# Attention in four joined pieces per unit, one piece per whole half step, and a fixed TensorE order in layer 1

## The chip, the cores and the metric

One core of a Trainium2 chip runs the whole program. The metric is the device time of one execution in microseconds; the time given for a kernel is the median of its runs.

## What is computed

Attention for 4 batches of 8 heads, 576 positions and head size 64, and behind it two feed-forward layers. The attention output of a head is the sum of two attentions: one over positions averaged by fours (144 of them), repeated four times, and one over a band of 7 positions around each query. The result, 2304 tokens by 512, goes through two layers with 2048 hidden columns each:

```python
out_d = sm_attn(q_d, k_d, v_d)                 # q, k, v averaged over 4 positions
out_up = np.repeat(out_d, factor, axis=2)
mask = np.abs(pos[:, None] - pos[None, :]) < factor
out_local = np.matmul(attn, v)                 # softmax over the masked scores
x = out_up + out_local
h = x @ w_in;  x = (h * sigmoid(1.702 * h)) @ w_out      # layer 1
h = x @ w_in;  x = elu(h) @ w_out                        # layer 2
```

All of it is float32. A product in float32 is made of three products of rounded halves (high by high, high by low, low by high), so each hidden block takes three matmuls where one would do.

## The kernel before

**Attention in units.** A unit is one batch and one pair of heads. There are 16; four of batch 0 are cut in two, and those and the four of batch 1 are computed in an opening whose order is written out token by token. This change is about the last eight, batches 2 and 3 (`rest[4:]`, called `turned`: their queries and keys are transposed on VectorE). A unit's work on TensorE is, by the names in the trace: `qk`, the banded scores in two PSUM tiles (5 and 4 windows); `qkd`, the averaged scores, two tiles; `pdt`, transposes of the averaged weights, two tiles; `ptr`, transposes of the banded weights, tiles of 4, 4 and 1 windows; `pvd`, averaged weights times values, one tile; `pv`, banded weights times values, two tiles (5 and 4 windows). VectorE masks and reduces the scores and adds the results into `x`, ScalarE takes the exponents (`exp_down` for `qkd`, three deferred groups of `exp_windows` for `qk`) and copies `pdT` and part of `PT`.

**PSUM.** In this part of the program every one of these tiles comes from the pool `spool`, tag `s`, which has two buffers, taken in turn. A tile can be written only when the tile two before it has been read by all its readers. For `qkd` the last readers are the exponents of `exp_down` on ScalarE (L630), which need `nmd`, made by two reductions (L609) and one scaling (L614) on VectorE.

**Layer 1 in steps.** Tokens go in blocks of 256 or 512; blocks 2 to 4 have 512 tokens and 16 steps each, a step being one column block f of 128 hidden columns. A step has two chunks: `products_h1` (12 matmuls of 128x512 into `h`, then tanh on ScalarE L1002, gate on VectorE L1006, rounding `g1h` L1012 and remainder `g1l` L1019) and `products_y1` of the step two before (12 matmuls into `y`). Each chunk is a generator that yields after each half of its matmuls. `step1` (L1276) goes through the chunks and at every yield calls `attend`, which first runs one deferred group of exponents and then one piece of attention from a queue:

```python
for chunk in chunks:
    for _ in chunk:
        ...
        with behind_step(si):
            for _ in range(rate(si)):
                attend()
```

So before there are four calls in a step. The queue is filled from `Unit.pieces` (L820 on): the front pieces of a unit (scores, averaged scores with `exps`, the transposing `turn` of the next unit), interleaved with the back pieces of the unit before (7 of them: `pdt` twice, `ptr` three times, `pv_down` with half of `pv`, the other half).

**What sets the order.** The code issues instructions in this order, and a scheduler of the language then places each engine's instructions by a model of when their operands are ready; `manual_schedule` keeps the written order for the engines that it names. The opening is under it for TensorE, ScalarE and VectorE. The steps behind it are under the scheduler for all engines, with `behind_step` (L953) as a bound: attention's instructions come behind the tanh and the gate of the last hidden block.

Of the kernel before, what the change touches and what calls it, by code (L numbers as in the profile page):

```python
# [24 lines left out]
NWIN = 9  # L25
# [10 lines left out]
FIRST = 4  # L36
# [9 lines left out]
}  # L46

RATE0 = 3
RATE1 = 1

LOADS = 6
NSIGN = 20
# [4 lines left out]
LAG = 2  # L57
# [51 lines left out]
OPENED = 16  # L109
# [9 lines left out]
def kernel(  # L119
# [275 lines left out]
    class Unit:  # L395
# [424 lines left out]
        def pieces(self):  # L820

            down = self.dn_from is None
            nxt = following.get(self)
            front = []
            if down and self not in turned:
                self.qkT, self.qkd = [None, None], [None, None]

                def k1():
                    self.trans(1, 1)
                    if nxt is not None and self not in early:  # L830
                        nxt.load_qk()

                front += [lambda: self.trans(0, 0), lambda: self.trans(0, 1), lambda: self.trans(1, 0), k1]
            elif not down:
                self.qkT = self.dn_from.qkT

            scores = [(lambda a=a: self.qk(a, min(a + 5, self.w1))) for a in range(self.w0, self.w1, 5)]
            if self in rest:
                scores = [lambda: (self.qk(0, 5), self.qk(5, self.w1))]
            front += scores  # L840
            if self in rest:
                front.append(lambda: (self.qk_down(0), self.qk_down(1), self.exps()))
                if nxt in turned:

                    front.append(nxt.turn)
                elif self in turned:
                    front.append(lambda: None)
            elif down:
                front += [lambda: self.qk_down(0), lambda: (self.qk_down(1), self.exps())]
            else:  # L850
                last = front.pop()
                front.append(lambda: (last(), self.exps()))

            def pv_last(a):
                self.pv(a, self.w1)
                if nxt is not None and self not in early:
                    nxt.load_v()

            back = []
            if down:  # L860
                back += [lambda: self.pdt(0), lambda: self.pdt(1)]
            back += [(lambda a=a: self.pt(a, min(a + 4, self.w1))) for a in range(self.w0, self.w1, 4)]
            starts = list(range(self.w0, self.w1, 5))
            if self in rest:
                back.append(lambda: (self.pv_down(), self.pv(0, 5)))
            else:
                if down:
                    back.append(self.pv_down)
                back += [(lambda a=a: self.pv(a, a + 5)) for a in starts[:-1]]
            back.append(lambda: pv_last(starts[-1]))  # L870
            return front, back

# [2 lines left out]
    rest = [Unit(b, hp, 0, NWIN) for b in range(1, B) for hp in range(NHP)]  # L875

    turned = rest[NHP:]
# [12 lines left out]
    back, back_of = [], None  # L890
# [9 lines left out]
    for u in rest[NREST:] + [None]:  # L900
        front, nback = pieces[u] if u is not None else ([], [])
# [11 lines left out]
        back, back_of = nback, u  # L913

    due = {}
# [27 lines left out]
    def split_some(blk):  # L943

        if blk < NBLK and nsplit[0] < NK * (blk + 1) and ready(blk):
            split_x(blk, nsplit[0] % NK)
            nsplit[0] += 1
# [4 lines left out]
    @contextmanager  # L952
    def behind_step(si):  # L953
        with ExitStack() as stack:
            if si >= WRITTEN:
                for ins in evacuated:
                    stack.enter_context(tc.issue_after(ins.ins))
            yield

    @contextmanager  # L960
    def behind_opening(si):
        with ExitStack() as stack:
            if si < OPENED + HELD:
                for ins in opened:
                    stack.enter_context(tc.issue_after(ins))
            yield
# [300 lines left out]
        released += [f"wo{f}" for f in (2 * (f2 - LAG), 2 * (f2 - LAG) + 1) if f >= 0]  # L1267
    used = set()

    def rate(si):  # L1270
        if due[1] and si < 8:
            return RATE0
        return RATE1

    waiting, prev, stage2, wextra = list(steps[OPENED - LAG:OPENED]), None, None, None
    def step1(si, blk, fs):  # L1276
        nonlocal prev, wt2, stage1, stage2, l1a, wextra, used
# [26 lines left out]
            hidden2(si - len(steps))  # L1304
        nchunk = 0
        for chunk in chunks:
            for _ in chunk:
                if not wt1.finished() and (blk == 0 or si < 3 * FIRST and si % 2 == 1):
                    wt1.convert()
                with behind_step(si):  # L1310
                    for _ in range(rate(si)):
                        attend()
                if blk == 0:
                    split_some(1)
                nchunk += 1
                if wt2 is not None and nchunk in (2, 3) and (nchunk == 2 or si % 2):
                    wt2.load(AHEAD + wt2.half - wt2.loaded)
                    with behind():
                        wt2.convert()
# [23 lines left out]
            wt2 = Weights(2, order2, stage2, 3, lambda tag: tag in used, 0)  # L1343
            wt2.load(AHEAD)

    for si, (blk, fs) in list(enumerate(steps + [(None, None)] * LAG))[OPENED:]:
        with behind_opening(si):
            step1(si, blk, fs)
    assert not queue
    l1.close()  # L1350

# [44 lines left out]
```

## Time and profile before

| | |
|---|---|
| time, 3 runs | 974.5, 975.35, 976.1 us (median 975.35) |
| profiled execution, own time | 974.49 us |
| span of that execution | 972.3 us |
| mean granted TensorE clock | 0.981 of full speed |
| busy: TensorE, VectorE, ScalarE, GpSimd | 948.0, 503.8, 466.6, 60.8 us |
| part with the units of batches 2 and 3 | about 195.5 to 376.9 us of the span |

How to read it: the profile comes from one execution. "PE" is TensorE's matmuls, "PEld" its weight loads, "DVE" VectorE, "ACT" ScalarE, "POOL" GpSimd. "L993" is line 993 of the kernel. In the views in order of time a row may stand for several like instructions (xN), and a matmul in float32 with plain operands (`qk`, `pv`, `ptr` and the like) appears as more than one record. Ends of matmuls are modelled; the distance between two starts is measured. Square brackets name what the engine waited for.

### The profile page before, as it was taken

Reading aid. Unit: us, or ns where it says so; the run is one execution under the profiler, and the core shown is the slowest. Engines: PE = TensorE matmul, PEld = TensorE weight load, DVE = VectorE, ACT = ScalarE, POOL = GpSimd, SP = SyncE. Lnnn points to the kernel's source line nnn. Section 1 sums busy time; section 2 is a strip of 40 time slices with the busy share of each in tenths; the row PEclk is TensorE's granted clock in tenths of the full one; section 3 lists DMA queues with packets and bytes.
Section 4 is the critical chain, followed back from the end, with each engine's and each line's share of the span. In section 5 each row is a group of like instructions: output and inputs, shape, how many; then the busy total and the mean of one; then the engine's idle time right before and its main releaser. Section 6 shows DMA issues by size and latency. Waiting matters only on the chain. (4 is left out here: it accounts for less than half of the span.)

```text
span 972.3 us, 14685 instructions
## 1 busy us (share of the span) xinstructions
PE 948.0 (97%) x5773; PEld 775.6 (80%) x5773; DVE 503.8 (52%) x900; ACT 466.6 (48%) x1115; POOL 60.8 (6%) x117
## 2 busy tenths in 40 slices
PE   8978999999999999999999999999999999999998
PEld 5758987777777778888888978877888888888897
DVE  5888997676654543223225898884223222322232
ACT  5667999464343532232225566664334333433343
POOL 4330110201111010000000000000000000000000
PEclk9588999999999999999999999999999999999999
DMA  9587712153222204010007921002001100100010
GB/s 192 162 232 205 232 31 55 46 116 64 52 55 46 70 20 144 1 43 1 1 1 240 366 88 43 1 12 77 1 1 38 39 1 1 55 0 1 1 44 22
DMA packets 113332, 67.97 MB, mean 70 GB/s; under 512 B 80752, under 2 KB 102768, under 8 KB 113264
## 3 DMA queue, kind: packets, MB, share of 16 engines
q1 hardware_dynamic: 110896, 66.46, 24.3%
q10 hardware_dynamic: 2368, 0.59, 0.4%
q8 instruction: 45, 0.74, 0.3%
q14 instruction: 23, 0.19, 0.1%
HBM read 57.59 MB, written 9.44 MB: 69 GB/s over the span
## 5 line engine op out<-in xcount | busy, mean ns | idle before, releaser
L1245 PE MATMUL o<-whl2o,g2h 128*128 128x512 f32 x576 | 181.0, 394 | 2.4 <-ACT ye L1072 2.1
L1196 PE MATMUL h<-x2h,whl2i 128*128 128x512 f32 (+1 forms) x640 | 159.3, 371 | 0.0
L1060 PE MATMUL y<-g1h,whl1o 128*128 128x512 f32 (+1 forms) x512 | 156.2, 371 | 0.0
L993 PE MATMUL h<-xh,whl1i 128*128 128x512 f32 (+1 forms) x640 | 147.1, 354 | 2.4 <-DVE g L1006 2.4
L1206 DVE SCALAR_TENSOR_TENSOR g<-e,h 128x512 f32<-128x512 f32 (+1 forms) x80 | 50.7, 634 | 177.9 <-ACT e L1204 177.6
L1196 PEld LDWEIGHTS h<-x2h,whl2i 128*128 128x128 f32 x640 | 114.7, 189 | 22.7
L1245 PEld LDWEIGHTS o<-whl2o,g2h 128*128 128x128 f32 x576 | 107.2, 189 | 27.1 <-ACT ye L1072 2.5
L993 PEld LDWEIGHTS h<-xh,whl1i 128*128 128x128 f32 x640 | 105.8, 190 | 19.4 <-DVE g L1006 3.3
L1203 ACT ACTIVATE e<-h 128x512 f32<-128x512 f32 (+1 forms) x80 | 44.3, 554 | 158.3 <-PE h L1196 158.3
L1245 PE MATMUL o<-whl2o,g2l 128*128 128x512 f32 x288 | 113.1, 393 | 0.0
L1060 PEld LDWEIGHTS y<-g1h,whl1o 128*128 128x128 f32 x512 | 92.4, 189 | 16.3 <-issue 1.2
L1006 DVE SCALAR_TENSOR_TENSOR g<-g,h 128x512 f32<-128x512 f32 x64 | 43.8, 684 | 118.9 <-ACT g L1002 118.9
L1002 ACT ACTIVATE g<-h 128x512 f32<-128x512 f32 x64 | 38.1, 596 | 122.7 <-PE h L993 115.9
L1060 PE MATMUL y<-g1l,whl1o 128*128 128x512 f32 (+1 forms) x256 | 93.7, 366 | 0.0
L1196 PE MATMUL h<-x2l,whl2i 128*128 128x512 f32 (+1 forms) x320 | 79.6, 370 | 0.0
L993 PE MATMUL h<-xl,whl1i 128*128 128x512 f32 (+1 forms) x320 | 77.6, 354 | 0.0
L1213 DVE TENSOR_TENSOR g2l<-g,g2h 128x512 fp32r<-128x512 f32 (+1 forms) x80 | 51.7, 646 | 36.8 <-ACT g2h L1211 21.6
L1211 ACT ACTIVATE g2h<-g 128x512 fp32r<-128x512 f32 (+1 forms) x80 | 47.1, 589 | 42.8 <-DVE g L1206 42.7
L1196 PEld LDWEIGHTS h<-x2l,whl2i 128*128 128x128 f32 x320 | 56.7, 188 | 11.0
L1245 PEld LDWEIGHTS o<-whl2o,g2l 128*128 128x128 f32 x288 | 54.4, 189 | 12.0
L993 PEld LDWEIGHTS h<-xl,whl1i 128*128 128x128 f32 x320 | 53.2, 191 | 7.3 <-issue 0.4
L1019 DVE TENSOR_TENSOR g1l<-g,g1h 128x512 fp32r<-128x512 f32 x64 | 44.2, 691 | 27.7 <-ACT g1h L1012 27.4
(128 smaller groups left out, 1326.2 us busy)
## 6 DMA issues: line engine op xcount, KB each, us to landing
wst1i<-in_moe_w_in_dram SPq DMA_DIRECT2D x16, 512.0 KB
wst1o<-in_moe_w_out_dram SPq DMA_DIRECT2D x16, 512.0 KB
wst2i<-in_moe_w_in_dram SPq DMA_DIRECT2D x16, 512.0 KB
wst2o<-in_moe_w_out_dram SPq DMA_DIRECT2D x16, 512.0 KB
vr<-in_v_dram SPq DMA_DIRECT2D x32, 144.0 KB
out_dram<-ot SPq DMA_DIRECT2D x18, 256.0 KB
y<-ydram SPq DMA_DIRECT2D x16, 256.0 KB
ydram<-ye SPq DMA_DIRECT2D x14, 256.0 KB
```

The source lines that it names most:

```text
L993: nc.tensor.matmul(out=hps[blk, fs][:, i, :], lhsT=w_in(1, f, c, wp), rhs=columns(xp, c), start=(n == 0), stop=(n >= len(todo) - nf), skip ...
L1002: return nc.scalar.activation(out=g, in_=hps[blk, fs], func=AF.Tanh, scale=0.851)
L1006: return nc.vector.scalar_tensor_tensor(out=g, in0=g, scalar=1.0, in1=ph, op0=ALU.add, op1=ALU.mult)
L1019: return nc.vector.tensor_tensor(out=gl, in0=g, in1=gh.bitcast(F32), op=ALU.subtract)
L1060: nc.tensor.matmul(out=sums(m), lhsT=w_out(1, f, wp)[:, m, :], rhs=gp[:, i, :], start=(opens and n == 0 and m % per == 0), stop=(last and ...
L1196: nc.tensor.matmul(out=ph[:, :n], lhsT=w_in(2, f, c, wp), rhs=xp[:, c, :n], start=(i == 0), stop=(i == 3 * NK - 1),)
L1203: nc.scalar.activation(out=e[:, :n], in_=ph[:, :n], func=AF.Relu, scale=-1.0)
L1206: urgent["dve"] = nc.vector.scalar_tensor_tensor(out=g[:, :n], in0=e[:, :n], scalar=-1.0, in1=ph[:, :n], op0=ALU.add, op1=ALU.max)
L1211: nc.scalar.activation(out=gh[:, :n], in_=g[:, :n], func=AF.Copy)
L1213: return lambda: nc.vector.tensor_tensor(out=gl[:, :n], in0=g[:, :n], in1=gh[:, :n].bitcast(F32), op=ALU.subtract)
L1245: nc.tensor.matmul(out=ops[bi][i], lhsT=gp[:, i * P:(i + 1) * P], rhs=wo[wp], start=(f == 0 and m == 0), stop=(f == NF - 1 and m == 2),)
```

## The change

The four parts: (1) a unit of batches 2 and 3 has two front pieces (`qk`; `qkd` with the exponents and the next unit's `turn`) and four back pieces (both `pdt`; `ptr` of 8 windows; `ptr` of the last window with `pvd`; all of `pv`), each of exactly two PSUM tiles. (2) `attend` is called once per chunk, behind its second half, so twice a step instead of four times. (3) The rate table and two calls that had nothing left to do in these steps (conversion of layer 1's weights, splitting of block 1) are gone. (4) All steps behind the opening are inside `manual_schedule` for TensorE: it keeps the written order, while ScalarE and VectorE are still placed by the scheduler.

```diff
@@ -44,9 +44,6 @@
     "qT": (3, "qs", 0), "sl": (3, "qs", 576),
     "kT": (4, "kd", 0), "qd": (4, "kd", 576), "kd": (4, "kd", 720),
 }
-
-RATE0 = 3
-RATE1 = 1
 
 LOADS = 6
 NSIGN = 20
@@ -839,12 +836,9 @@
                 scores = [lambda: (self.qk(0, 5), self.qk(5, self.w1))]
             front += scores
             if self in rest:
-                front.append(lambda: (self.qk_down(0), self.qk_down(1), self.exps()))
-                if nxt in turned:
-
-                    front.append(nxt.turn)
-                elif self in turned:
-                    front.append(lambda: None)
+                front.append(
+                    lambda: (self.qk_down(0), self.qk_down(1), self.exps(), nxt.turn() if nxt in turned else None)
+                )
             elif down:
                 front += [lambda: self.qk_down(0), lambda: (self.qk_down(1), self.exps())]
             else:
@@ -856,17 +850,19 @@
                 if nxt is not None and self not in early:
                     nxt.load_v()
 
+            if self in rest:
+                return front, [
+                    lambda: (self.pdt(0), self.pdt(1)), lambda: (self.pt(0, 4), self.pt(4, 8)),
+                    lambda: (self.pt(8, NWIN), self.pv_down()), lambda: (self.pv(0, 5), pv_last(5)),
+                ]
             back = []
             if down:
                 back += [lambda: self.pdt(0), lambda: self.pdt(1)]
             back += [(lambda a=a: self.pt(a, min(a + 4, self.w1))) for a in range(self.w0, self.w1, 4)]
             starts = list(range(self.w0, self.w1, 5))
-            if self in rest:
-                back.append(lambda: (self.pv_down(), self.pv(0, 5)))
-            else:
-                if down:
-                    back.append(self.pv_down)
-                back += [(lambda a=a: self.pv(a, a + 5)) for a in starts[:-1]]
+            if down:
+                back.append(self.pv_down)
+            back += [(lambda a=a: self.pv(a, a + 5)) for a in starts[:-1]]
             back.append(lambda: pv_last(starts[-1]))
             return front, back
 
@@ -1267,11 +1263,6 @@
         released += [f"wo{f}" for f in (2 * (f2 - LAG), 2 * (f2 - LAG) + 1) if f >= 0]
     used = set()
 
-    def rate(si):
-        if due[1] and si < 8:
-            return RATE0
-        return RATE1
-
     waiting, prev, stage2, wextra = list(steps[OPENED - LAG:OPENED]), None, None, None
     def step1(si, blk, fs):
         nonlocal prev, wt2, stage1, stage2, l1a, wextra, used
@@ -1304,14 +1295,10 @@
             hidden2(si - len(steps))
         nchunk = 0
         for chunk in chunks:
-            for _ in chunk:
-                if not wt1.finished() and (blk == 0 or si < 3 * FIRST and si % 2 == 1):
-                    wt1.convert()
-                with behind_step(si):
-                    for _ in range(rate(si)):
+            for half, _ in enumerate(chunk):
+                if half == 1:
+                    with behind_step(si):
                         attend()
-                if blk == 0:
-                    split_some(1)
                 nchunk += 1
                 if wt2 is not None and nchunk in (2, 3) and (nchunk == 2 or si % 2):
                     wt2.load(AHEAD + wt2.half - wt2.loaded)
@@ -1343,9 +1330,10 @@
             wt2 = Weights(2, order2, stage2, 3, lambda tag: tag in used, 0)
             wt2.load(AHEAD)
 
-    for si, (blk, fs) in list(enumerate(steps + [(None, None)] * LAG))[OPENED:]:
-        with behind_opening(si):
-            step1(si, blk, fs)
+    with tc.manual_schedule(engines={ET.PE}):
+        for si, (blk, fs) in list(enumerate(steps + [(None, None)] * LAG))[OPENED:]:
+            with behind_opening(si):
+                step1(si, blk, fs)
     assert not queue
     l1.close()
 
```

How the order moves, at three places. A name such as `pdt_2_2_0_3357` is tile, batch, pair of heads, first window and a buffer number; `h_2_8` is block 2, step 8.

TensorE, unit 2 of batch 2, from the last matmuls of the y chunk behind that unit's successor's `qkd`. Before:

```order
L1060 MATMUL y_2_2880<-g1h_4_3061,whl1o_1471 128x512
L1060 MATMUL y_2_2880<-g1l_4_3063,whl1o_1471 128x512
L1060 MATMUL y_2_2880<-g1h_4_3061,whl1o_1471 128x512
L993 MATMUL h_2_7_3300<-xh_2588,whl1i_1220 128x512 x2
L686 MATMUL pdt_2_2_0_3294<-ident,pd_2_0_3010 72x72 x4
L993 MATMUL h_2_7_3300<-xh_2588,whl1i_1220 128x512 x2
L993 MATMUL h_2_7_3300<-xl_2589,whl1i_1220 128x512 x2
L686 MATMUL pdt_2_2_0_3314<-ident,pd_2_0_3010 72x72 x4
L993 MATMUL h_2_7_3300<-xl_2589,whl1i_1220 128x512 x2
L993 MATMUL h_2_7_3300<-xh_2588,whl1i_1220 128x512 x4
```

With the change:

```order
L1056 MATMUL y_2_2841<-g1h_6_3140,whl1o_1652 128x512
L1056 MATMUL y_2_2842<-g1h_6_3140,whl1o_1652 128x512
L1056 MATMUL y_2_2842<-g1l_6_3142,whl1o_1652 128x512
L1056 MATMUL y_2_2842<-g1h_6_3140,whl1o_1652 128x512
L683 MATMUL pdt_2_2_0_3357<-ident,pd_2_0_3064 72x72 x4
L683 MATMUL pdt_2_2_0_3363<-ident,pd_2_0_3064 72x72 x4
L989 MATMUL h_2_9_3369<-xh_2590,whl1i_1456 128x512 x4
L989 MATMUL h_2_9_3369<-xl_2591,whl1i_1456 128x512 x4
L989 MATMUL h_2_9_3369<-xh_2590,whl1i_1456 128x512 x4
L701 MATMUL ptr_2_2_0_3393<-ident,sl_2_0_3017 70x128 x4
L701 MATMUL ptr_2_2_0_3399<-ident,sl_2_0_3017 70x128 x4
```

Before, each `pdt` stands alone between matmuls of the next `h`; now both stand together in front of the whole `h`, and both `ptr` tiles together behind it.

VectorE, from the gate of the hidden block that ends just ahead of `qkd` of unit 3 of batch 2 (its maxima `nmd`, the next unit's `qT` and `kT`). Before:

```order
L1006 SCALAR_TENSOR_TENSOR g_2_6_3235<-g_2_6_3235,h_2_6_3196 128x512
L609 TENSOR_REDUCE nmd_3_0_3242<-qkd_2_3_0_3244 72x2
L609 TENSOR_REDUCE nmd_3_0_3242<-qkd_2_3_0_3248 72x2
L1019 TENSOR_TENSOR g1l_6_3240<-g_2_6_3235,g1h_6_3238 128x512
L614 TENSOR_SCALAR nmd_3_0_3242<-nmd_3_0_3242 72x4
L532 STREAM_TRANSPOSE qT_0_0_3266<-rawq_0_0_3042 128x576
L522 TENSOR_REDUCE qd_0_0_3270<-qT_0_0_3266 128x144
```

With the change:

```order
L1002 SCALAR_TENSOR_TENSOR g_2_8_3301<-g_2_8_3301,h_2_8_3288 128x512
L606 TENSOR_REDUCE nmd_3_0_3308<-qkd_2_3_0_3310 72x2
L606 TENSOR_REDUCE nmd_3_0_3308<-qkd_2_3_0_3314 72x2
L529 STREAM_TRANSPOSE qT_0_0_3323<-rawq_0_0_3086 128x576
L1015 TENSOR_TENSOR g1l_8_3306<-g_2_8_3301,g1h_8_3304 128x512
L611 TENSOR_SCALAR nmd_3_0_3308<-nmd_3_0_3308 72x4
L529 STREAM_TRANSPOSE kT_0_0_3325<-rawk_0_0_3091 128x576
```

The transpose of the next unit's queries has moved ahead of the remainder `g1l` and of the scaling of `nmd`.

ScalarE, the first hidden block of block 3 (`pd` are the exponents that read `qkd`). Before (the exponents of this unit stand ahead of these rows):

```order
L1002 ACTIVATE g_3_0_4084<-h_3_0_4061 128x512
L623 ACTIVATE sl_2_0_3985,sumset<-sl_2_0_3985,nm_2_0_3986 128x70 x3
L1012 ACTIVATE g1h_0_4087<-g_3_0_4084 128x512
L694 ACTIVATE pdT_1_0_4071<-pdt_3_1_0_4098 72x288
L1002 ACTIVATE g_3_1_4124<-h_3_1_4104 128x512
L711 ACTIVATE PT_1_0_4111<-ptr_3_1_0_4131 70x512
L1002 ACTIVATE g_3_2_4153<-h_3_2_4137 128x512
```

With the change:

```order
L998 ACTIVATE g_3_0_4050<-h_3_0_4037 128x512
L998 ACTIVATE g_3_1_4093<-h_3_1_4080 128x512
L620 ACTIVATE sl_2_0_4011,sumset<-sl_2_0_4011,nm_2_0_4012 128x70
L1008 ACTIVATE g1h_0_4053<-g_3_0_4050 128x512
L620 ACTIVATE sl_2_0_4011,sumset<-sl_2_0_4011,nm_2_0_4012 128x70 x2
L627 ACTIVATE pd_2_0_4058,sumset<-qkd_3_2_0_4059,nmd_2_0_4057 72x144 x2
L627 ACTIVATE pd_2_0_4058,sumset<-qkd_3_2_0_4063,nmd_2_0_4057 72x144 x2
L691 ACTIVATE pdT_1_0_4103<-pdt_3_1_0_4104 72x288
```

The tanh of the second hidden block now stands ahead of the first block's rounding and of the four exponents that read `qkd`.

## Rows read from the trace of the kernel before

**Rows 1.** The page, part 1: TensorE's busy time, share of span, instructions.
```profile
PE 948.0 (97%) x5773; PEld 775.6 (80%) x5773; DVE 503.8 (52%) x900; ACT 466.6 (48%) x1115; POOL 60.8 (6%) x117
```

**Rows 2.** Stretches: busy time (instructions) by engine, then TensorE's clock, DMA.
```profile
195.50:376.90 181.40, 179.25 (x1377) 136.34 (x1378) 103.66 (x203) 81.44 (x298) 18.68 (x36) 1.00 0.27 58
400.00:500.00 100.00, 100.00 (x443) 82.81 (x442) 27.06 (x40) 26.52 (x45) 0.00 (x0) 1.00 0.03 11
```

**Rows 3.** Waits of TensorE, 195 to 377 us: total, times, longest.
```profile
PE h L993 <- DVE g L1006: 1.3, 2, 1.0
PE pdt L686 <- ACT pd L630: 0.5, 1, 0.5
PE qkd L602 <- DVE sl L577: 0.2, 1, 0.2
```

**Rows 4.** TensorE in order of time: start us, duration us, operation, count.
```profile
231.07 0.48 PE L1060 MATMUL y<-g1h,whl1o 128*128 128x512 f32 x1
231.38 0.40 PE L1060 MATMUL y<-g1l,whl1o 128*128 128x512 f32 x1
...
238.74 0.40 PE L1060 MATMUL y<-g1l,whl1o 128*128 128x512 f32 x1
239.07 0.33 PE L741 MATMUL pv<-PT,vw 70*64 70x64 f32 x2
239.32 0.73 PE L1060 MATMUL y<-g1h,whl1o 128*128 128x512 f32 x2
239.89 0.40 PE L1060 MATMUL y<-g1l,whl1o 128*128 128x512 f32 x1
```

**Rows 5.** Three engines in order of time, 246.5 to 251.8 us.
```profile
246.51 0.72 PE L602 MATMUL qkd<-kd,qd 64*72 64x144 f32 x8
...
246.96 0.60 ACT L1002 ACTIVATE g<-h 128x512 f32<-128x512 f32 x1 [8.14 <-PE h L993]
...
247.45 0.34 ACT L623 ACTIVATE sl<-sl,nm 128x70 f32<-128x70 f32 x1
...
248.19 0.81 DVE L609 TENSOR_REDUCE nmd<-qkd 72x2 f32<-72x288 f32 x2
...
248.46 0.62 ACT L1012 ACTIVATE g1h<-g 128x512 fp32r<-128x512 f32 x1
...
249.11 0.69 DVE L1019 TENSOR_TENSOR g1l<-g,g1h 128x512 fp32r<-128x512 f32 x1
...
249.72 0.43 DVE L614 TENSOR_SCALAR nmd<-nmd 72x4 f32<-72x4 f32 x1
...
250.04 0.61 PE L993 MATMUL h<-xh,whl1i 128*128 128x512 f32 x2
...
250.24 0.38 ACT L630 ACTIVATE pd<-qkd,nmd 72x144 f32<-72x144 f32 x1 [0.15 <-DVE nmd L614]
...
250.88 0.19 ACT L630 ACTIVATION_READ_ACCUMULATOR pd<-qkd,nmd 72x1 f32 x1
...
251.12 0.44 PE L686 MATMUL pdt<-ident,pd 72*72 72x72 f32 x4 [0.47 <-ACT pd L630]
...
251.59 0.20 ACT L630 ACTIVATION_READ_ACCUMULATOR pd<-qkd,nmd 72x1 f32 x1
```

**Rows 6.** VectorE by shape, 230 to 380 us: busy us, mean ns.
```profile
L532 DVE STREAM_TRANSPOSE qT<-rawq 128x576 f32<-128x576 f32 x4 | 3.1, 770 | 0.0
```

**Rows 7.** Order of time around the first unit of batch 2.
```profile
205.60 1.32 PE L559 MATMUL qk<-kT,qT 64*64 64x70 f32 x36
...
205.92 0.60 ACT L1002 ACTIVATE g<-h 128x512 f32<-128x512 f32 x1 [1.31 <-DMA ydram<-ye_both]
```

**Rows 8.** TensorE at the start of layer 2's output products.
```profile
576.48 0.73 PE L1245 MATMUL o<-whl2o,g2h 128*128 128x512 f32 x2 [2.07 <-ACT ye L1072]
```

**Rows 9.** Two stretches behind that wait, columns as in rows 2.
```profile
578.00:580.00 2.00, 2.00 (x6) 1.62 (x5) 1.86 (x3) 1.65 (x4) 0.00 (x0) 0.50 0.60 158
580.00:582.00 2.00, 2.00 (x7) 1.55 (x7) 2.00 (x5) 1.69 (x3) 0.00 (x0) 0.66 0.23 36
```

## The prediction

> **What bounds the kernel now.** The page's first part comes first: TensorE is busy for 97% of the span, VectorE and ScalarE for about half [rows 1]. So every microsecond that TensorE loses or gains counts, and nothing else does. Next the stretches: where only layer 1 runs, 100 us hold 443 matmuls of 128x512, 0.226 us each, with no idle time, and nothing can be won there; where the units of batches 2 and 3 are mixed in, 181.4 us of span, TensorE shows 179.25 us of work, while VectorE works 103.66 and ScalarE 81.44 us [rows 2]. Then the waits in that stretch: four in all, 2.0 us together [rows 3]. The reader is to see that waits are almost nothing today. What the stretch costs is attention's own matmuls and the changes between them and the dense matmuls.
>
> All times below are taken from the start of a piece on TensorE, and the sum is made against the profiled execution's own 974.49 us; the median of the runs is 975.35, 0.86 us above it, and the predicted time is moved up by that.
>
> **Term A: fewer changes of work on TensorE.** Counted in the order of time, TensorE turns to attention 83 times between 195.5 and 376.9 us. With six pieces in each of eight units it does so 48 times, 35 fewer. What one costs: behind four transposes (`pdt`) the two following dense matmuls start 0.31 us apart, 0.09 more than the 0.226 of an undisturbed pair; around two records of `pv` the start comes 0.33 us after a dense matmul (0.10 more) and the next two dense ones take 0.57 (0.12 more), so 0.22 [rows 4]. 35 times 0.09 is 3.2 us, 35 times 0.22 is 7.7. About half of the removed ones are transposes; I take 5 us gained.
>
> Here the row is at odds with a rule. The late start behind a piece is that of a dense matmul whose weights were not there yet. The Trainium skill (TensorE: Matmul & The Clock Gate, "Step-by-step: what each phase is for") says that TensorE pulls the next weight load ahead of the matmuls in flight where the row groups don't conflict or the load goes to the background buffer; by that a change would be hidden, term A would be nothing, and the kernel 5 us slower than I say. The rows price each change above zero, so I keep them.
>
> **Term B: the waits of before.** They hang on the old places of the pieces. All four go at most: 2.0 us gained [rows 3]; none goes at least. The places of the wait on `pd` and those on the gate are new, so I take 2.0.
>
> **Term C: new waits for the two PSUM buffers.** This decides. Every piece now fills both buffers of the pool, and TensorE keeps the written order, so it stands still until both are read. For five of the six pieces the readers are quick. Behind `qkd` they are not: its tiles are last read by four exponents on ScalarE, which need `nmd` scaled on VectorE, and on VectorE that scaling stands behind the gate, two reductions and the remainder `g1l`. The same chain stands in the trace of before [rows 5]: `qkd` starts at 246.51; the tanh of the block just finished at 246.96; the reductions at 248.19, `g1l` at 249.11, the scaling at 249.72 to 250.15; the exponents from 250.24. The second one's reading ends at 251.07, and `pdt` starts at 251.12, 4.61 us after `qkd`, having waited 0.47. With the change the transpose of the next unit's queries stands ahead of `g1l`, and takes 0.77 [rows 6]: 5.38. TensorE gets there after `qkd` and twelve dense matmuls, as it did at 250.04, 3.53 after [rows 5]. So it waits 1.8 us, and then again: the second buffer is free with the fourth exponent (251.79 in the rows, 0.72 after the second), while the first four transposes take only some 0.25. That is 0.47 more, 2.25 us a time.
>
> - Five times in this way (behind `qkd` of units 1 to 3 of batch 2, 0 and 1 of batch 3): 11.3 us. The first of them waits also for the weighing of unit 0; I add nothing for that.
> - Behind `qkd` of the last unit there is nothing to transpose: 2.25 less 0.77, 1.5 us.
> - Behind the first `qkd` (unit 0 of batch 2) the following piece is the next `qk`. Its tanh cannot start before 205.92, since its tile's last content is still on its way to memory [rows 7]; that wait is not on TensorE and stays. From there, by the durations of rows 5 and 6: tanh 0.60 and gate 0.69 to 207.2, reductions to 208.1, transpose to 208.8, `g1l` to 209.5, scaling to 210.0, two exponents with the reading (0.83) to 210.8. TensorE has the same work ahead of it as before and is there at 205.60 [rows 7]: 5.2 us.
> - In block 3 `qkd` of unit 2 is followed by a hidden chunk, and the tanh of that second block stands ahead of everything that the exponents need. It starts 3.53 plus 0.45 after `qkd`; then 0.60, one exponent 0.34, `g1h` 0.62, `g1l` 0.69, scaling 0.43, two exponents 0.83 [rows 5]: 7.5, less 3.53 is 4.0, with the second buffer 4.5 us.
>
> Together 22.5 us. Below: with the scaling placed as early as in the trace of before, 0.47 for the first buffer and 0.47 for the second, eight times, 7.5 us. Above: some 3 us more if the weighing of unit 0 and the second buffer in the first case bind. I take 22.5, since the order of the three engines is known and each duration has a row.
>
> **Term D: the clock.** A wait of 2.07 us on TensorE is in the trace of before [rows 8]. Behind it the granted clock was 0.50, 1.2 GHz, for 2 us, in which six matmuls stood instead of nine, and 0.66 on the mean of the next 2 [rows 9], which is 1.4 us more at the low level: of 3.4 us at half speed about 1.6 are lost. No wait of [rows 3], the longest 1.0, was followed by that: the clock there is 1.00 [rows 2]. The two waits of 4 us and over are longer than 2.07: 3.2 us. For the other six, 1.8 us with a short second one, the rows don't say: nothing at least, 9.6 us more at most. I take nothing, as none of them is 2.07 in one piece.
>
> Removing the rate table and the two calls costs and gains nothing: they issue no instruction in these steps. DMAs are the same in number. On SP's queue the four writes of block 0 and 1's result now stand together ahead of the next unit's queries, and the loads of values follow their pieces; the queries are needed three steps later, some 22 us, which covers them. If a load came late, `turn` would wait on VectorE, and with it the gate behind it.
>
> Sum: 974.5 - 5 - 2 + 22.5 + 3.2 = 993.2 us, and 994 against the median.
>
> **Rivals.** *The chain fits, and the kernel is faster.* VectorE is idle for 43% and ScalarE for 55% of the stretch [rows 2], so the buffers might be free when TensorE comes; then only A and B are left, 975.35 - 7 = 968 us. The point is whether the way from `qkd` to a free buffer is under 3.5 us. Against it: it was 4.6 before, without the transpose in it [rows 5]. *Half the waits.* The two long ones shrink to the regular size because engines at the head of a batch have run ahead, some regular ones to 1.8, and the clock stays up: 975.35 - 7 + 17 = 985 us. For it: TensorE's clock stayed at 1.00 through all of [rows 3]. *Every wait lowers the clock*: six times 1.6 more, 1004 us; for it, 1.8 and 0.47 us with a quarter of a microsecond of small transposes between them are close to the 2.07 of [rows 8]. *The change does not do what it says*: the written order might be undone, or the old one be as good as it; the printed order of TensorE has the joined pieces where the code puts them, so this is small: 975 us.
>
> **How the numbers follow.** The forecast, 988 to 999 us, has a chance of 0.40; half the waits 0.25; every wait with a low clock 0.19; faster 0.12; no change 0.04. 0.2%, 2 us, is about what a measurement of this kernel can tell from no change. The range is 978 to 1004: it leaves out the faster case, no change, and the far side of the low-clock case, about 0.2. Slower by over 0.2% is 0.84.
>
> **What would show it.** In the waits of TensorE `pdt` waiting for `pd` on ScalarE should appear seven times, most of 1.5 to 2 us in the first part and some 0.4 in the second, and `qk` for `pd` or `kT` once with about 5; attention should stand in 48 stretches; the granted clock should dip behind the two longest waits. It is wrong if `pdt` starts within 3.6 us of `qkd`, if the stretches between the pieces don't get shorter, or if the time beyond 400 us of the span changes other than by a shift.

## The result, and the profile after

The changed kernel takes 987.89 us, the median of four runs (987.49 to 989.49); the kernel before took 975.73 in the runs beside it. The ratio is 1.0129, 95% interval 1.0112 to 1.0147: slower, as forecast, inside the range, and 6 us below the point. The profiled execution took 987.54 us, its span is 985.8.

The page's first part, of the kernel after [rows 1]: TensorE's busy time is 2.3 us less than before, and its share is smaller.

```profile
PE 945.7 (96%) x5773; PEld 776.2 (79%) x5773; DVE 499.8 (51%) x900; ACT 466.7 (47%) x1115; POOL 67.1 (7%) x117
```

Stretches of the kernel after, columns as in [rows 2]. The one with the units of batches 2 and 3 is 199.5 us long, of which TensorE stands idle for 15.5 (2.2 before). The one behind it is as before: 0.226 us a matmul.

```profile
195.50:395.00 199.50, 184.04 (x1368) 142.91 (x1367) 103.93 (x208) 82.45 (x299) 25.57 (x36) 0.97 0.25 54
410.00:500.00 90.00, 90.00 (x399) 74.53 (x398) 24.70 (x37) 24.55 (x41) 0.00 (x0) 1.00 0.06 22
```

Waits of TensorE between 190 and 400 us in the kernel after, columns as in [rows 3]. All are for the readers of `qkd` or for the weighing of `pd` (VectorE multiplies the exponents by one over their sums, L662); the waits of before for the gate and for `sl` are gone.

```profile
PE pdt L683 <- ACT pd L627: 8.8, 12, 3.2
PE qk L556 <- ACT pd L627: 4.9, 1, 4.9
PE pdt L683 <- DVE pd L662: 1.8, 1, 1.8
```

One of the four regular places, in order of time [rows 5]. The transpose of the next unit's queries and `g1l` stand ahead of the scaling (248.25), the exponents follow at 248.50, and `pdt` starts at 249.38, 4.52 us after `qkd`, then waits again for the fourth exponent.

```profile
244.86 0.72 PE L599 MATMUL qkd<-kd,qd 64*72 64x144 f32 x8
245.03 0.60 ACT L998 ACTIVATE g<-h 128x512 f32<-128x512 f32 x1 [6.24 <-PE h L989]
...
246.26 0.81 DVE L606 TENSOR_REDUCE nmd<-qkd 72x2 f32<-72x288 f32 x2
...
246.53 0.62 ACT L1008 ACTIVATE g1h<-g 128x512 fp32r<-128x512 f32 x1
...
246.99 0.77 DVE L529 STREAM_TRANSPOSE qT<-rawq 128x576 f32<-128x576 f32 x1
247.68 0.64 DVE L1015 TENSOR_TENSOR g1l<-g,g1h 128x512 fp32r<-128x512 f32 x1
...
248.25 0.15 DVE L611 TENSOR_SCALAR nmd<-nmd 72x4 f32<-72x4 f32 x1
248.50 0.38 ACT L627 ACTIVATE pd<-qkd,nmd 72x144 f32<-72x144 f32 x1 [1.35 <-DVE nmd L611]
249.14 0.19 ACT L627 ACTIVATION_READ_ACCUMULATOR pd<-qkd,nmd 72x1 f32 x1
...
249.38 0.44 PE L683 MATMUL pdt<-ident,pd 72*72 72x72 f32 x4 [0.86 <-ACT pd L627]
...
250.10 0.44 PE L683 MATMUL pdt<-ident,pd 72*72 72x72 f32 x4 [0.28 <-ACT pd L627]
```

Where the time went. Between the same dense matmuls of both traces, one late in the opening and one behind the attention, the span grew by 12.3 us. The opening of this execution was 3.1 us longer (a load of values came later), and behind the attention it was 1.9 shorter; a second profile of the changed kernel (below) has the opening 1.0 shorter than before and the stretch 12.6 longer. So the opening is scatter, and the stretch is the change. The part behind the attention differs mainly by the clock: before, it fell behind the wait at the start of layer 2's output products [rows 8, 9]; in both profiles of the changed kernel it stayed at full speed there, behind 1.92 us in the first and 2.07 in the second (the rows of the second are in the last section).

In the stretch, attention's price is the distance between starts of dense matmuls over 0.227 us, added up: 58.5 us in 83 stretches before, 70.6 in 48 after. Of these 3.3 and 21.8 are waits and low clock; the pieces themselves cost 55.2 before and 48.8 (6.1 a unit) after.

### The profile page after: what moved, and what is told of

It reads as the page before. It is cut to its first block, busy times and chain, and to the rows that moved or that the text cites. A ratio compares the mean times of both kernels' runs of the same rounds, so it can differ in the third digit from the quotient of the medians.

```text
span 985.8 us, 14672 instructions
## 1 busy us (share of the span) xinstructions
PE 945.7 (96%) x5773; PEld 776.2 (79%) x5773; DVE 499.8 (51%) x900; ACT 466.7 (47%) x1115; POOL 67.1 (7%) x117
## 5 line engine op out<-in xcount | busy, mean ns | idle before, releaser
L1056 PE MATMUL y<-g1h,whl1o 128*128 128x512 f32 (+1 forms) x512 | 152.5, 368 | 0.0
L1192 PEld LDWEIGHTS h<-x2h,whl2i 128*128 128x128 f32 x640 | 114.3, 188 | 22.5
L989 PE MATMUL h<-xl,whl1i 128*128 128x512 f32 (+1 forms) x320 | 74.5, 353 | 0.0
L989 PEld LDWEIGHTS h<-xl,whl1i 128*128 128x128 f32 x320 | 55.5, 194 | 8.4
```

The source lines that it names most:

```text
L989: nc.tensor.matmul(out=hps[blk, fs][:, i, :], lhsT=w_in(1, f, c, wp), rhs=columns(xp, c), start=(n == 0), stop=(n >= len(todo) - nf), skip ...
L1056: nc.tensor.matmul(out=sums(m), lhsT=w_out(1, f, wp)[:, m, :], rhs=gp[:, i, :], start=(opens and n == 0 and m % per == 0), stop=(last and ...
L1192: nc.tensor.matmul(out=ph[:, :n], lhsT=w_in(2, f, c, wp), rhs=xp[:, c, :n], start=(i == 0), stop=(i == 3 * NK - 1),)
```

## The experiments

The runs beside the kernel before had its median at 974.6 to 976.0 us; ratios are to those runs. Profiled executions have their own time, so stretches are compared, not spans.

**1. The scheduler places TensorE again.** Joined pieces and half rate kept.

```diff
-    with tc.manual_schedule(engines={ET.PE}):
-        for si, (blk, fs) in list(enumerate(steps + [(None, None)] * LAG))[OPENED:]:
+    for si, (blk, fs) in list(enumerate(steps + [(None, None)] * LAG))[OPENED:]:
...
```

> The changed kernel (987.9 us) with the written order of TensorE taken away: the joined pieces, one per half step, are placed by the scheduler, which puts the transposes of the averaged weights 4 to 7 dense matmuls (0.9 to 1.6 us) later and the second qk 6 later; 54 stretches of attention in place of 48. Theory (TensorE stands still for the two PSUM buffers behind qkd, and only because the written order lets nothing pass): the four regular waits of 1.5 us, the 2.0 of the second unit and the 1.1 of the last one go, 1.4 us each of the two long ones go: 976 us, 973 to 979. Rival (joined pieces or the half rate cost the time themselves): 986 to 989 us.

Measured: 974.87 us, ratio 1.0001 (0.9985 to 1.0018). The theory's number: joined pieces and half rate together cost nothing on balance. They still make 5.5 us of waits (2.0 before), with the low clock behind the one of 1.9, and win that back on the pieces: `pv` now stands whole, 36 records, in every unit (last line). Its waits between 195 and 420 us, and one `pv`:

```profile
PE pdt L683 <- ACT pd L627: 2.1, 2, 1.9
PE h L989 <- DVE g L1002: 2.0, 1, 2.0
PE qk L556 <- ACT pd L627: 1.3, 1, 1.3
PE pdt L683 <- DVE pd L662: 0.2, 1, 0.2
```

```profile
227.19 1.27 PE L738 MATMUL pv<-PT,vw 70*64 70x64 f32 x36
```

**2. Written order alone, with the old pieces and four calls.**

```diff
-    for si, (blk, fs) in list(enumerate(steps + [(None, None)] * LAG))[OPENED:]:
...
+    with tc.manual_schedule(engines={ET.PE}):
+        for si, (blk, fs) in list(enumerate(steps + [(None, None)] * LAG))[OPENED:]:
...
```

> The kernel before (975.7 us) with only the written TensorE order through layer 1 added: seven back pieces, four calls a step, 72 stretches of attention by its order, 12 dense matmuls between qkd and the first transposes of averaged weights as in the changed kernel, 6 more to the second. Theory (written order makes the wait): some six to eight waits of 0.9 to 1.5 us come in on the first buffer, none on the second, two longer ones at the first unit and in block 3, less 1.4 for eleven stretches and 3 for the old waits: 982 us, 978 to 986. Rival (it needs the joined pieces to make the waits, the order alone is harmless): 974 to 976 us.

Measured: 972.09 us, ratio 0.9964 (0.9950 to 0.9978): faster than before, and both numbers were wrong. Waits come in, as the theory has it, but fewer (first fence), and the written order gains something that neither theory had: it cuts the pieces less. One unit's `pv` on TensorE, by start: before, in stretches of 2, 2, 4 and 28 records (second fence); here in 20 and 16 (third); in the changed kernel in one of 36 (fourth).

```profile
PE pdt L686 <- ACT pd L630: 3.0, 4, 1.1
PE qk L559 <- DVE kT L532: 2.0, 2, 1.6
```

```profile
259.85 0.28 PE L741 MATMUL pv<-PT,vw 70*64 70x64 f32 x2
...
261.64 0.33 PE L741 MATMUL pv<-PT,vw 70*64 70x64 f32 x2
...
263.49 0.34 PE L741 MATMUL pv<-PT,vw 70*64 70x64 f32 x4
...
265.11 1.15 PE L741 MATMUL pv<-PT,vw 70*64 70x64 f32 x28
```

```profile
261.31 0.75 PE L741 MATMUL pv<-PT,vw 70*64 70x64 f32 x20
...
263.57 0.69 PE L741 MATMUL pv<-PT,vw 70*64 70x64 f32 x16
```

```profile
260.61 1.27 PE L738 MATMUL pv<-PT,vw 70*64 70x64 f32 x36
```

A stretch of two records delays the dense matmuls by 0.36 us and the pair behind it by 0.11, while two records within a whole `pv` cost 0.07 (1.29 over 36, twice). Without their waits the old pieces, whole, cost 6.2 us a unit, the joined ones 6.1.

**3. The scaling on ScalarE.** Taken out of VectorE's queue.

```diff
         def down_scale(self):
+            if self in turned:
+                nc.scalar.activation(out=self.nmd, in_=self.nmd, func=AF.Copy, scale=self.scale_down())
+                return
```

> The changed kernel with the scaling of nmd moved from VectorE, where it stands behind a transpose and g1l, to ScalarE, right ahead of the exponents that read it (one more small instruction there per unit). Theory (the chain over VectorE's queue sets when the buffers come free): the exponents start about 1.1 us earlier at a regular place, as TensorE arrives, so the four regular waits of 1.5 and the last unit's 1.1 nearly vanish (0 to 0.2 each), the two long ones lose about 1 each, the second unit's 2.0 (weighing) stays: 979 us, 977 to 982. Rival (something else is late, the tanh or ScalarE's own queue): 986 to 988 us.

Measured: 982.02 us, ratio 1.0068 (1.0049 to 1.0088), 3 us above the expected time, at the edge of its range, and 4 below the rival's. By starts the four regular waits fell from 1.52 to 0.36 us each and the last unit's from 1.07 to 0.36: the chain over VectorE is what made them. But neither long wait lost the 1 us expected: the first stayed at 5.0, with another name, and block 3's at 3.1. At the second unit the wait for the weighing grew (1.8 to 2.5 of idle time) and now had the low clock behind it. In the stretch, 11.0 us longer than before, only 1.3 of the changed kernel's 12.3 are won:

```profile
PE qk L556 <- DVE kT L529: 5.0, 1, 5.0
PE pdt L686 <- ACT pd L630: 4.2, 7, 3.1
PE pdt L686 <- DVE pd L665: 2.5, 1, 2.5
```

**4. An empty piece behind `qkd`,** for every unit but the first.

```diff
         pending = [(p, None) for p in back]
+        if pending and u in turned:
+            queue.append((lambda: None, None))
         if pending:
```

> The changed kernel with one empty piece behind qkd of every unit but the first: TensorE has 24 dense matmuls in place of 12 between qkd and the transposes of the averaged weights. Nothing is computed otherwise; 48 stretches. Theory: all waits but the first unit's (6.3 with its low clock, plus 1.2 more at the low clock) go, with the low clock behind the block-3 wait: 1.5 x 4 + 2.0 + 5.3 + 1.1 = 14.4 us less, 973.5 us, 971 to 976. Rival (the joined pieces, half rate or written order have costs beyond those waits, or the waits come back at the next piece): 982 us or more.

Measured: 977.28 us, ratio 1.0023 (1.0010 to 1.0036), 1.3 us above the expected range. Every wait behind the seven `qkd` went. Two were left: the first unit's (4.8 us), and a new one of 3.0 at the head of block 3, where `ptr` needs the buffer that the copy of `pdT` reads, and that copy stands on ScalarE behind a tanh and two copies of the finished y, which wait for earlier copies to reach memory:

```profile
326.48 1.21 ACT L1070 ACTIVATE ye<-y 128x512 f32<-128x512 f32 x2 [3.16 <-DMA ydram<-ye]
329.22 0.60 ACT L1000 ACTIVATE g<-h 128x512 f32<-128x512 f32 x1 [1.53 <-DMA ydram<-ye]
...
331.25 0.68 ACT L691 ACTIVATE pdT<-pdt 72x288 f32<-72x288 f32 x2
331.69 1.43 PE L701 MATMUL ptr<-ident,sl 128*70 128x128 f32 x8 [3.02 <-ACT pdT L691]
```

**5. The changed kernel again,** without an edit, for the scatter.

> The changed kernel once more, beside the next three on one chip. Its profile showed 12.3 us more than before in the stretch with the joined pieces, 3.1 more in the opening, where nothing was changed (a load of values came later), and 1.9 less behind it. Theory A (opening and tail are scatter between executions): the ratio to before is 1.011 to 1.013 again, but the profile's opening is within 1.5 us of that of before. Theory B (the longer opening belongs to the change): the profile shows the 3 us in the opening again.

Measured: 984.12 us, ratio 1.0109 (1.0081 to 1.0138). Theory A: the opening is 1.0 us shorter than that of before, the stretch 12.6 longer, the waits the same to 0.2 us.

**6. y into the dead x tile.** So that ScalarE never waits for a write of y.

```diff
-                    t = gpool.tile([P, 512], F32, tag="g", name=f"ye{m // per}_{blk}", bufs=2)
+                    t = gpool.tile([P, 512], F32, tag="g", name=f"ye{m // per}_{blk}", bufs=2) if blk == NBLK - 2 else \
+                        x32[2 if blk == BOTH else blk + 1][:, m // per, :]
```

> The changed kernel, with the finished y of a block copied into the dead x tile of the next block in place of a buffer of g, so that no copy and no tanh waits for a write to memory. Theory (at the two block ends ScalarE stands 6 to 8 us for the writes of y, and that makes the two long waits): the first unit's wait (5.9, with 1.4 for the low clock behind it) and that in block 3 (4.1, with 1.2) fall to the 1.5 of a regular place, and the granted clock stays up: 9.5 us less than the changed kernel, 978 us, 976 to 980. Rival (it is the order of the chain, tanh and exponents of a second block ahead, as the prediction had it): at most 2 us less, 985 us or more.

Measured: 989.65 us, ratio 1.0152 (1.0133 to 1.0171): no gain, in the rival's range; the stretch is 13.6 us longer than before. The theory was half of it. The exponents on the first `qkd` were done by 208.0, and TensorE still stood to 211.5 at the second unit's `qk`, now for `kT`: in this kernel the scheduler put the transpose of the keys behind the second hidden block's gate and remainder (second fence), where the changed kernel has it right behind the scaling (third). And at the head of block 3 the edit made a wait of its own, since block 5's x tile takes the place that y is read from:

```profile
PE qk L556 <- DVE kT L529: 4.4, 1, 4.4
PE qkd L599 <- DVE x L753: 3.4, 1, 3.4
```

```profile
210.00 0.69 DVE L1015 TENSOR_TENSOR g1l<-g,g1h 128x512 fp32r<-128x512 f32 x1 [0.84 <-ACT g1h L1008]
210.61 0.77 DVE L529 STREAM_TRANSPOSE kT<-rawk 128x576 f32<-128x576 f32 x1
```

```profile
212.48 0.16 DVE L611 TENSOR_SCALAR nmd<-nmd 72x4 f32<-72x4 f32 x1
212.55 0.77 DVE L529 STREAM_TRANSPOSE kT<-rawk 128x576 f32<-128x576 f32 x1
```

The same edit in the kernel before:

> The kernel before with the same copy of y into the dead x tile, nothing else. Theory (before, the scheduler places the pieces where ScalarE's stand for the write costs little): the waits of 1.3 us at the head of block 2 and 1.1 at the head of block 3 go, 973 us, 972 to 975. Rival (the copy of y is what the kernel hangs on, whatever the order of TensorE): 5 us or more gained, below 970 us.

Measured: 974.09 us, ratio 1.0003 (0.9983 to 1.0023): inside the theory's range, but no gain. The waits went as it has it, none of over 0.15 us is left in the stretch; the scheduler cut the pieces in other places, and the stretch is 0.9 us longer than before.

**7. Both edits, with empty pieces behind every `qkd`.** The line of experiment 6, and against experiment 4:

```diff
-        if pending and u in turned:
+        if u in turned:
             queue.append((lambda: None, None))
```

> The changed kernel with both: y copied into the dead x tile, and an empty piece behind qkd of every unit, the first too. Theory (every microsecond that the change lost is a wait for the two PSUM buffers behind qkd, or the clock behind such a wait): no wait of over 0.3 us and no low clock in the stretch, 48.8 us for 48 pieces plus 1.5 of scatter between dense matmuls, where the kernel before has 59.9 in all: 9.6 us less than before, 965.5 us, 964 to 968. Rival (the waits come back at the next place, as one did behind the empty piece at the end of block 2): 970 us or more.

Measured: 973.24 us, ratio 0.9981 (0.9965 to 0.9997): a little faster than before, but in the rival's range. One wait was left in the stretch, with the low clock behind it. VectorE had the transpose of the keys behind two gates, two remainders and a weighing; nothing held it up where it stood:

```profile
PE qk L556 <- DVE kT L529: 5.3, 1, 5.3
```

```profile
213.48 0.77 DVE L529 STREAM_TRANSPOSE kT<-rawk 128x576 f32<-128x576 f32 x1
```

**8. VectorE in written order too,** in blocks 2 and 3, with y in the x tile and, beside it, with y in `g`. Both keep the empty pieces of experiment 7.

```diff
-    with tc.manual_schedule(engines={ET.PE}):
...
+    todo = list(enumerate(steps + [(None, None)] * LAG))[OPENED:]
+    cut = next(n for n, (_, (blk, _)) in enumerate(todo) if blk == 4)
+    for part, engines in ((todo[:cut], {ET.PE, ET.DVE}), (todo[cut:], {ET.PE})):
+        with tc.manual_schedule(engines=engines):
...
```

> The kernel with empty pieces behind every qkd and y copied into the dead x tile, and in blocks 2 and 3 VectorE too in written order. In the run without that, one wait was left, 5.3 us at the second unit's qk for kT: its keys lay in SBUF some 8 us earlier, and VectorE had the transpose behind two gates, two remainders and a weighing, where the scheduler had put it. Theory (the place of that transpose in VectorE's queue makes the last wait): kT is ready about 2 us before TensorE comes, no wait of over 0.3 us and no low clock in the stretch, 7.5 us less: 965.5 us, 963.5 to 968. Rival (the keys' load itself is late, or written order on VectorE brings waits of its own at gates): 970 us or more.

> The same with y copied into buffers of g, as in the kernels before and after the change: tells what the write of y costs once the rest is out of the way. Theory (ScalarE stands for the write at both block ends, and with it tanh, gate and exponents): TensorE waits 2 to 5 us at the head of block 2, for the gate or the exponents of the first qkd, and some 3 us at the head of block 3, with low clock behind one or both: 6 to 10 us more than the kernel with y in the x tile, 971 to 976 us. Rival (with empty pieces the writes are hidden): the same as that kernel within 1.5 us.

Measured: 987.68 us, ratio 1.0123 (1.0098 to 1.0147), and 987.91, ratio 1.0123 (1.0093 to 1.0152). The wait for `kT` went in the first, but the rival held: four new waits came, for the copy of `PT`, which in written order stands behind a gate, a remainder and the weighing. They hide what y costs, so the second run told nothing on that.

```profile
PE pvd L717 <- DVE PT L706: 9.7, 4, 4.3
PE qkd L599 <- DVE sl L574: 2.7, 2, 2.5
```

**9. One bound instead:** the next gates of block 2 come behind the transpose of the second unit's keys. Again with the empty pieces, and with y in the x tile and with y in `g`. (`held[:blk == 2]` is the whole list in block 2 and empty elsewhere.)

```diff
             for which in range(2):
                 self.qkT[which] = self.t([P, S], ("qT", "kT")[which])
-                nc.vector.transpose(out=self.qkT[which], in_=self.raw[which].rearrange("p t d -> p (t d)"))
+                last = nc.vector.transpose(out=self.qkT[which], in_=self.raw[which].rearrange("p t d -> p (t d)"))
+            if self is turned[1]:
+                held.append(last)
...
     def h_gate(blk, fs):
+        with ExitStack() as stack:
+            for ins in held[:blk == 2]:
+                stack.enter_context(tc.issue_after(ins.ins))
...
```

> Empty pieces behind every qkd and y in the dead x tile, VectorE placed by the scheduler again, with one bound: the gates of block 2 that follow come behind the transpose of the second unit's keys. Theory (that transpose's place in VectorE's queue is the last wait of the run with both edits, 5.3 us at the second qk and the low clock behind it): no wait of over 0.3 us and no low clock in the stretch, 48 stretches that cost 48.8 us, some 9.5 us less in the stretch than the kernel before: 0.990 to 0.993 of its time, 965.5 to 968 us. Rival (another wait takes its place): 970 us or more.

Measured: 965.71 us, ratio 0.9906 (0.9873 to 0.9940): faster than both kernels, the time that was expected. The stretch is 7.8 us shorter than before, 1.7 less than written ahead, with 0.9 of waits left, one of them of 0.7, where none of over 0.3 was expected; the pieces cost 48.8. Its waits and the stretch:

```profile
PE qkd L601 <- DVE sl L576: 0.9, 2, 0.7
```

```profile
195.50:377.00 181.50, 180.60 (x1333) 142.76 (x1332) 99.38 (x197) 80.25 (x291) 21.50 (x36) 1.00 0.26 56
```

> The same with y copied into buffers of g as in the kernels before and after. Theory (ScalarE's stand for the write of y at the block ends is what made the two long waits): TensorE waits 1.5 to 4 us at the head of block 2 (gate of the first hidden block, exponents of the first qkd) and about 3 us at the head of block 3, with the low clock behind at least one: 5 to 8 us more than the kernel with y in the x tile, 971 to 975 us. Rival (the empty pieces hide the writes): within 1.5 us of that kernel.

Measured: 968.64 us, ratio 0.9928 (0.9905 to 0.9951), 2.9 us more than with y in the x tile, between the two. At the head of block 2 one wait of 1.9 us for the gate was left, with low clock behind it; at the head of block 3 none: there the empty pieces hide the write.

```profile
PE h L993 <- DVE g L1011: 1.9, 1, 1.9
```

## Why the prediction was right, and 6 us too high

The sign and the mechanism held: two PSUM buffers, both filled by each piece, a written order that lets nothing pass, and a late reader behind `qkd`. Experiments 1 and 2 show that the loss takes both parts: without the written order it is gone, and without the joined pieces and the half rate the written order gains. Either part alone still makes 5.5 and 5.0 us of waits; together they make 15.5. Which of joined pieces and half rate it needs was not taken apart. Seven `pdt` waited (six for the exponents, the second unit's for the weighing) and one `qk`, attention stood in 48 stretches, the clock fell behind the two longest waits only, as forecast. One sign failed in size: at a regular place the two parts of the wait were 0.86 and 0.28 us of idle time, where 1.5 to 2 and some 0.4 were to be seen. Another, that the time beyond 400 us would only shift, was not met either; the 1.9 us there are the clock of [rows 9], which belongs to the profile of before and not to the change. The sum was 18.7 us for the stretch, and 12.3 were measured, and every term was off; most of the 6 us are term C:

- **Term A, taken as 5 gained, was 6.4**, and for another reason than I gave. I priced a change of work at 0.09 to 0.22 us. Whole pieces show 24 fewer changes (72 stretches in experiment 2, 48 after) worth 0.8 us, 0.03 each. The other 5.6 come with `qk` and `pv` left whole or nearly so: my row of 0.22 [rows 4] was the price of a cut `pv`, not of a change. Either part of the change does this, the written order in experiment 2 (two stretches) and the joined pieces in experiment 1 (one), so the 5.6 belong to neither alone. The Trainium skill (TensorE: Matmul & The Clock Gate, "Step-by-step: what each phase is for") has the next weight load pulled ahead of matmuls in flight, where its conditions hold. For joining alone the 0.03 is nearer to that than my prices were.
- **Term B, taken as 2.0, was 3.3**: by the distances between starts the old waits cost more than the idle time that [rows 3] gives.
- **Term C, taken as 22.5, was 17.9.** Here the step failed that added the transpose's whole 0.77 to a chain copied from before with its durations. Three things make nearly all of the 0.86 us that `pdt` came earlier, 4.52 after `qkd` in place of 5.38. First, in [rows 5] `g1l` starts at 249.11, 0.03 after its `g1h` ended: the chain of before had a wait in it. With the transpose in front, `g1h` (246.53 to 247.15) was long done at 247.68, and from reductions to `g1l` it took 1.42 us, 0.50 more than before and not 0.77. Second, the tanh started 0.17 us after `qkd` and not 0.45. Third, the exponents came 0.25 us behind the start of the scaling and not 0.52. So a regular place cost 1.5 us (forecast 2.25), the last unit 1.1 (1.5), the second 2.0 (2.25; it waits for the weighing, to which I had added nothing). The first unit's 5.0 (5.2) and block 3's 3.8 (4.5) came out close. For block 3 the chain was told in part: the second hidden block's tanh does stand ahead of the first block's `g1h`, and `g1l` waits for that (last row). But ScalarE also stood there for the writes of y, which I had seen at block 2 alone, and with it the tanh and the gate of the first hidden block, so that VectorE came to `g1l` only 0.18 us before `g1h` was done. There were two chains, about as long:

```profile
340.99 1.33 ACT L1068 ACTIVATE ye<-y 128x512 f32<-128x512 f32 x2 [4.44 <-DMA ydram<-ye]
343.74 0.60 ACT L998 ACTIVATE g<-h 128x512 f32<-128x512 f32 x1 [1.42 <-DMA ydram<-ye]
...
346.65 0.69 DVE L1015 TENSOR_TENSOR g1l<-g,g1h 128x512 fp32r<-128x512 f32 x1 [0.18 <-ACT g1h L1008]
```

- And it was told too short for the first unit, whose following piece needs the transposed keys as well as a buffer. The transpose of the keys and the second exponent's reading end at 213.3 and 213.5 us there. Both come late through one front, the tanh that stands for the writes of y and VectorE's queue behind it, and part only behind the scaling. In experiment 3 they ended 0.1 us apart again. Experiment 6 made the exponents early, but the keys' transpose came into a later place. The wait at that `qk` went only where an empty piece gave the exponents time and the keys' transpose stood early: in both kernels of experiment 9 (with y in `g`, 1.9 us for the gate are left) and in the first of experiment 8, where 2.7 us for `sl` came a piece later.
- **Term D, taken as 3.2, was 3.9:** 2.4 behind the first wait, where `qk` itself still ran at the low clock, and 1.5 behind the other. Nothing behind the waits of up to 1.8, as forecast; that was in part luck, since a wait of 1.81 us had the low clock behind it in experiment 8 (last section).

Of the rivals, *half the waits* (985 us) lay nearer to the time than the forecast; the waits were not half, but the regular ones were two thirds of their size, and against that rival the clock did fall. *The chain fits* needed a way of under 3.5 us; it was 4.5. Its number, 968, is about what the kernel reaches once the waits are taken away (968.6 and 965.7 in experiment 9, which have further edits), so the gain that it named was there, behind the waits. What stays open: what the write of y costs the changed kernel by itself, since experiment 6 made a wait of its own, and experiment 9 shows its price (2.9 us, from four and seven runs whose times overlap) only where the empty pieces already hide a part.

## What to carry to other kernels

A fixed order on one engine is only as good as the places of its operands' makers on the others: before fixing TensorE, look where each reader of a small PSUM pool stands in VectorE's and ScalarE's queues, and leave a step between a tile and its slow reader. Do not sum a chain from durations alone where a row in it has a wait: what is put in front may run in that wait. And when a cause of a wait is taken away and the time stays, look which other operand of the same instruction came last, and whether the scheduler has moved its maker, before giving the theory up.

## What the runs showed of the hardware

The length of a wait does not decide alone whether the clock falls behind it. All fourteen profiles have a wait at the same instruction, the start of layer 2's output products. Six show 1.2 GHz behind it, with waits of 1.88 to 2.61 us; eight show the full 2.4, with waits of 1.28 to 3.00. Waits of 2.07 us came both ways, with the low clock before [rows 8, 9] and without it in experiment 5 (first fence); the 3.00 of experiment 4 had none behind it (second fence). The part of the span behind the attention goes with this: it is within 0.4 us of that of before in the six, and 1.3 to 2.2 us shorter in the eight. In the first kernel of experiment 8 a wait of 1.81 us for `PT` came three times; the first (from 290.6) had no low clock behind it, the second (from 343.2) and the third over 3 us of it (third fence, the first two). So a forecast of such a loss is a chance, not a sum. The stretches have their columns as in [rows 2]:

```profile
588.19 0.73 PE L1241 MATMUL o<-whl2o,g2h 128*128 128x512 f32 x2 [2.07 <-ACT ye L1068]
...
588.00:590.00 2.00, 1.81 (x8) 1.50 (x9) 2.00 (x4) 1.08 (x3) 0.00 (x0) 1.00 0.76 203
```

```profile
579.83 0.73 PE L1243 MATMUL o<-whl2o,g2h 128*128 128x512 f32 x2 [3.00 <-ACT ye L1070]
...
580.00:582.00 2.00, 2.00 (x9) 1.62 (x10) 1.97 (x5) 1.31 (x3) 0.00 (x0) 1.00 0.71 172
```

```profile
292.00:296.00 4.00, 3.55 (x20) 2.65 (x20) 0.50 (x2) 0.29 (x1) 1.38 (x3) 1.00 0.06 8
...
345.00:349.00 4.00, 3.97 (x16) 3.12 (x17) 0.08 (x1) 0.29 (x1) 1.36 (x3) 0.59 0.00 0
```
